# Batch 0 of an attention and expert kernel: offsets placed behind the sums of q, two scalings and a cast moved to GpSimd, an eviction to ScalarE

## The chip, the core and the metric

One core of a Trainium2 chip runs the whole kernel. TensorE (PE), VectorE (DVE), ScalarE (ACT), GpSimd (POOL) and SyncE (SP, which only issues transfers here) each work through their own list of instructions in order and wait for each other by semaphores. The metric is device microseconds (us) of one execution, lower is better. The kernel before takes 192.34 us, the median of three runs (192.24 to 192.36).

## What is computed

Linear attention over 8 batches of 8 heads, 576 rows of 64, and a mixture of 8 experts behind it, of which each row goes through one:

```python
q_s = exp(q - max(q)); q_s = q_s / (sum(q_s, -1) + 1e-09)        # over the head's 64 columns
k_s = exp(k - max(k)); k_s = k_s / (sum(k_s, over rows) + 1e-09)
kv  = einsum('bhsd,bhse->bhde', k_s, v)
x   = einsum('bhsd,bhde->bhse', q_s, kv)                          # -> 4608 rows of 512
logits = x @ w_gate + modality_bias[modality_id]
e_idx  = argmax(logits); gate = softmax(logits)[e_idx]
out[rows of e] = gate * (relu(x @ w1[e]) @ w2[e])
```

The biases make two experts win, one for each modality, and the kernel sorts rows by modality: rows of the first kind (side a) fill `xs` from the front, rows of the other (side b) from the back. A check at the end redoes rows if that was not so.

## The kernel before

**The stages of a batch.** ACT takes the exponential of q in place (`eq`, in two halves of the heads), DVE sums it over 64 columns (`sq`, L914), inverts the sums (`iq`, L925 and L926), and five instructions scale q into bf16 (`nq`, L930: four of 128x512 and one of 128x256, named by the first of their columns of rows: 0, 2, 4, 6, 8). ACT takes the exponential of k (`ekk`, L941); two instructions cast v to bf16 (`cv`, L951). TensorE multiplies k and v (`kv`, L1044, two parts), DVE scales the products into `kvbd` (`ki`, `kb`, L1071 to L1080). TensorE transposes and sorts the scaled q with a permutation (`s1`, L1130; the permutation `perm`, L959, is made by DVE), ACT or DVE evicts each group (`ev`, L1142 or L1144, into `et`), TensorE multiplies by `kvbd` (`s2`, L1169), and `put` (L1200) copies 64 columns at a time to their places in `xs`, on ACT for side a and on DVE for side b in the first two batches.

**The offsets.** Where a column group begins in `xs` is data: `off_run` scans the counts of side a (`ahead_n`, a part of the PSUM tile `own`) and packs the offsets into `offp` (L706 to L723); `lo0` loads them into registers of ACT and DVE (L1097); `aoff_run` copies `ahead_n` to SBUF (L727) for GpSimd, which can only then make the bias table (`bsel`, L757 to L762) and the places of rows (`slot`, L733 to L738).

**The experts.** For side a and b in turn, TensorE makes logits (`lg`, L1246), the hidden layer (`h`, L1318; L1312 clears a bank for the first one, which is split in two) and the output (`y`, L1331). The weights (`W`) come by transfers that GpSimd issues (`wi00` to `wi03` for the first expert, L533 and L544; `wi10` to `wi13` for the second), the first of them not before q of batch 1 has landed. q, k and v come by SP's queue.

**What sets the order.** `Plan.order` runs a small model of the engines with a cost for each step and the table `TUNED` of priorities; out of it comes one list, in which every step has an engine and a planned start, and the list is written out as it stands. A step keeps its place behind the steps ahead of it on its engine's list. `pl.fill` puts matmuls that nobody reads (fillers, L1599) into TensorE's planned gaps before 38 us, which keep that engine busy:

```python
for o in started:
    if o.engine == "PE" and o.start < hi:
        left = o.start - free - spare
        while left > 0:
            out.append(filler)
            left -= each * (2 if o.start - spare - left < slow else 1)
        free = max(free, o.start + o.costs["PE"][0])
    out.append(o)
```

Of the kernel before, what the change touches and what calls it, by code (L numbers as in the profile page):

```python
# [16 lines left out]
ACT = mybir.ActivationFunctionType  # L17
# [13 lines left out]
def view(t, dims, off=0, parts=None):  # L31
    p0 = t.ap[0]
    if parts is None:
        return bass.AP(tensor=t.tensor, offset=t.offset + off, ap=[list(p0)] + [list(d) for d in dims])
    lo, n = parts
    return bass.AP(
        tensor=t.tensor, offset=t.offset + lo * p0[0] + off, ap=[[p0[0], n]] + [list(d) for d in dims]
    )
# [206 lines left out]
def kernel(  # L245
# [12 lines left out]
    nc = tc.nc  # L258
# [26 lines left out]
    def sb(shape, dtype, name):  # L285
        return pool.tile(shape, dtype, name=name)

    pl = Plan()
# [4 lines left out]
    n_st, n_ps, n_hT, n_y = 5, 7, 3, 6  # L293
# [15 lines left out]
    ahead_n = own[:, P + 2 * NJ * HG : P + 2 * NJ * HG + NC + 1]  # L309
    sums = [own[:, P + i * NJ * HG : P + (i + 1) * NJ * HG] for i in range(2)]  # L310

    r_st, r_ps = Ring(n_st), Ring(n_ps - 1)
# [173 lines left out]
    key = sb([P, 2], FP32, "key")  # L486
# [159 lines left out]
    aoff = sb([P, NC + 1], FP32, "aoff")  # L646
# [16 lines left out]
    bsel = sb([P, NSL, E], FP32, "bsel")  # L663
# [39 lines left out]
    def off_run(_):  # L703
        d = nc.vector
        r = ps_t[r_buf.idx]
        d.tensor_tensor_scan(  # L706
            out=ahead_n[:, 1 : NC + 1],
            data0=ones[:, 0:NC],
            data1=r[:, NC : 2 * NC],
            initial=0.0,  # L710
            op0=ALU.mult,
            op1=ALU.add,
        )
        d.tensor_copy(out=off_i, in_=ahead_n[0:1, 0:NC])
        d.scalar_tensor_tensor(
            out=offp[:, :, 0:4],
            in0=view(off_i, [[NJ, B], [2, 4]], 1),
            scalar=16,
            in1=view(off_i, [[NJ, B], [2, 4]]),
            op0=ALU.logical_shift_left,  # L720
            op1=ALU.bitwise_or,
        )
        d.tensor_copy(out=offp[:, :, 4], in_=view(ahead_n, [[NJ, B]], NJ - 1, (0, 1)))  # L723

    def aoff_run(e):
        if e == "ACT":
            nc.scalar.copy(out=aoff, in_=ahead_n)  # L727
        else:
            nc.vector.tensor_copy(out=aoff, in_=ahead_n)

    def slot_run(_):
        d = nc.gpsimd
# [113 lines left out]
    pl.follow(wg_t, o_rank)  # L846
    o_pos = pl.op({"DVE": (0.8, 0.9)}, pos_run, [o_rank, c_dve], key="pos", rank=-6, uses=[r_buf])
    o_off = pl.op({"DVE": (0.8, 1.0)}, off_run, [o_pos], key="off", rank=-5, uses=[r_buf])
    o_aoff = pl.op({**on_dve(NC), **on_act(NC)}, aoff_run, [o_off], key="aoff", rank=3)
    o_vals = pl.op({"DVE": (0.7, 0.85, True)}, vals_run, [c_dve2], key="vals", rank=14)  # L850
    o_slot = pl.op({"POOL": (1.65, 1.75, True)}, slot_run, [o_aoff], key="slot", rank=12)
# [743 lines left out]
    quiet = 38.0  # L1595
# [6 lines left out]

    with tc.manual_schedule():
        waiting = []
        for o in pl.fill(pl.order({r_ps: (quiet, n_ps - 1)}), 4.5, quiet, 0.3, 0.216, 12.7, Op({"PE": (0.216, 0.45)}, unread)):
            o.run(o.engine)
            if o.engine == "PE" and waiting:
                waiting.pop()(None)
            if o in second:
                waiting.append(second[o])  # L1610
# [7 lines left out]
    def keys():  # L1618
# [12 lines left out]
    n_ps = ps_t[0]  # L1631
# [5 lines left out]
        out=ok[:, 0:1], in0=n_ps[0:1, 0:1], scalar1=float(N) - 0.5, scalar2=None, op0=ALU.is_ge  # L1637
# [5 lines left out]
        out=ok[:, B : 2 * B - 1], in0=need, scalar=(S - 2 * P) / (2 * P), in1=so_far, op0=ALU.mult, op1=ALU.is_ge  # L1643
    )
    for i, (limit, op) in enumerate(((MID - RW, ALU.is_ge), (N - (MID - RW), ALU.is_le))):
        nc.vector.tensor_scalar(
            out=ok[:, 2 * B - 1 + i : 2 * B + i], in0=aoff_x[0:1, NC : NC + 1], scalar1=float(limit), scalar2=None, op0=op
# [5 lines left out]
        out=nrest, in0=okm, scalar1=-float(E), scalar2=float(E), op0=ALU.mult, op1=ALU.add  # L1653
# [11 lines left out]
    with tc.For_i(0, nr) as e:  # L1665
        first = nc.vector.tensor_copy(out=kcol, in_=view(wrow, [[1, 1]], e))
# [8 lines left out]
        for kd in range(KD):  # L1675
            for h2 in range(2):
                nc.sync.dma_start(
                    out=st[kd // 2][64 * h2 : 64 * h2 + 64, (kd % 2) * F : (kd % 2 + 1) * F],
                    in_=bass.AP(
                        tensor=moe_w1.tensor,  # L1680
                        offset=e * (D * F) + (4 * (kd % 2) + 2 * h2 + kd // 2) * Dh * F,
                        ap=[[F, Dh], [1, F]],
                    ),
# [3 lines left out]
        for part in range(2):  # L1687
            nc.sync.dma_start(
                out=view(st[2 + part], [[D, 4], [1, D]]),
                in_=bass.AP(  # L1690
                    tensor=moe_w2.tensor, offset=e * (F * D) + part * 4 * P * D, ap=[[D, P], [P * D, 4], [1, D]]
                ),
            )
            nc.vector.tensor_copy(
                out=W[:, 0, W2 + part * 4 * D : W2 + (part + 1) * 4 * D], in_=st[2 + part][:, 0 : 4 * D]
            )
        with tc.For_i(0, NSL) as c:
            d = nc.vector
# [3 lines left out]
            for kd in range(KD):  # L1702
                nc.tensor.matmul(
                    out=ps_t[4][:, 0:E], lhsT=xx[:, kd, :], rhs=wg_sb[:, kd, :], start=(kd == 0), stop=(kd == KD - 1)
# [12 lines left out]
            for f in range(KF):  # L1717
                for kd in range(KD):
                    nc.tensor.matmul(
                        out=ps_t[f % 3][:, 0:P],  # L1720
# [39 lines left out]
```

## Time and profile before

| | |
|---|---|
| median of three runs | 192.34 us |
| the profiled execution's own time | 192.32 us |
| its span, first to last instruction | 190.7 us |
| TensorE matmul busy | 176.8 us, 93% of the span |
| VectorE busy | 143.7 us, 75% |
| ScalarE busy | 126.6 us, 66% |
| GpSimd busy | 101.8 us, 53% |
| mean granted TensorE clock | 0.991 |

The profile gives for each engine when an instruction began and how long it took. Shares of the whole span say little about one stage; the change touches the stretch from 9 to 30 us alone, so the timelines of that stretch are what to read, engine by engine, with the time that an engine stood idle before a row in brackets and who ended it.

### The profile page before, as it was taken

The page shows a single profiled execution, that of the slowest core. Times are in us where ns is not written, and L with a number is a line of the kernel's source. Part 1 is how long each engine was busy: PE and PEld are TensorE (multiplying, and loading weights), DVE is VectorE, ACT ScalarE, POOL GpSimd, SP SyncE. Part 2 cuts the span into 40 slices and gives each one's busy share as a digit, 9 for nine tenths or more (in the row PEclk, how much of TensorE's full clock was granted, in tenths as well). Part 3 has the DMA queues.
Part 4 walks back from the last instruction along what each step waited for, and adds up shares of the span by engine and source line. Part 5 has one row for each costly group of instructions (what it writes and reads, how often), then busy time and mean ns, then how long its engine had stood idle before and what let it go on. Part 6 is the DMA issues. An engine that isn't in the chain of part 4 may idle for free.

```text
span 190.7 us, 4965 instructions
## 1 busy us (share of the span) xinstructions
PE 176.8 (93%) x1743; PEld 123.7 (65%) x1759; DVE 143.7 (75%) x381; ACT 126.6 (66%) x251; POOL 101.8 (53%) x130
## 2 busy tenths in 40 slices
PE   1889799999999999999999999999999999999970
PEld 0535458587794687579668865895895975664740
DVE  4798987999989686659889899796596764363750
ACT  2655996989657299999899697599589971100000
POOL 7048989096817749844738924554831204504441
PEclk9999999999999999999999999999999999999996
DMA  5999999999999999999996683100210301412202
GB/s 196 331 401 391 270 177 213 221 375 366 195 336 383 398 410 409 397 402 406 354 389 221 258 302 115 55 5 0 111 59 0 115 0 55 168 55 110 98 31 100
DMA packets 18077, 42.34 MB, mean 222 GB/s; under 512 B 1393, under 2 KB 1393, under 8 KB 18050
## 3 DMA queue, kind: packets, MB, share of 16 engines
q1 hardware_dynamic: 12816, 28.31, 40.7%
q0 software_dynamic: 5200, 13.64, 24.8%
q8 instruction: 14, 0.23, 0.5%
q10 hardware_dynamic: 34, 0.05, 0.2%
q14 instruction: 13, 0.11, 0.2%
HBM read 36.75 MB, written 9.70 MB: 244 GB/s over the span
## 4 chain that ended last, share of the span: by engine, by line
PE 82%; DMA 7%; ACT 4%; DVE 3%; issue 2%; POOL 1%; ACTq 0%
PE ps L1318 33%; PE ps L1331 32%; DMA st<-in_v_dram 5%; PE ps L1044 5%; PE ps L1130 4%; PE ps L1169 3%; PE ps L1246 2%; DMA mraw<-in_moe_modality_id_dram 1%; ACT vb L951 1%; ACT xs L1200 1%; PE ps L1484 1%; ACT et L1142 1%; PE ps L1515 1%; DVE own L914 1%; PE ps L808 1%
## 5 line engine op out<-in xcount | busy, mean ns | idle before, releaser
L1318 PE MATMUL ps<-xs,W 128*128 128x256 bf16 x576 | 68.4, 273 | 0.1
L1331 PE MATMUL ps<-W,hT 128*128 128x512 bf16 (+1 forms) x281 | 64.8, 373 | 0.9
L1291 POOL DMA_INDIRECT out_dram<-y_sb,idx x36 | 35.5, 986 | 52.9 <-DVE y_sb L1288 39.9
L1318 PEld LDWEIGHTS <-W 128*128 128x128 bf16 x576 | 54.4, 98 | 7.7 <-issue 1.4
L1331 PEld LDWEIGHTS <-hT 128*128 128x128 bf16 x296 | 28.2, 98 | 29.1 <-issue 0.2
L930 POOL TENSOR_TENSOR eq<-st,qi 128x512 bf16<-128x512 f32 (+1 forms) x38 | 36.0, 973 | 12.1 <-PE ps L1169 4.5
L1288 DVE TENSOR_SCALAR y_sb<-ps,gate 128x512 f32<-128x512 f32 (+1 forms) x30 | 22.0, 732 | 19.5 <-PE ps L1331 14.8
L1200 ACT CAST xs<-ps 128x256 f32 (+1 forms) x90 | 28.8, 437 | 2.6 <-PE ps L1169 1.1
L1282 DVE TENSOR_SCALAR hT<-ps 128x512 bf16<-128x512 f32 x35 | 23.8, 686 | 5.4 <-PE ps L1318 3.8
L914 DVE TENSOR_REDUCE own<-st 128x18 f32<-128x1152 f32 x16 | 21.7, 1355 | 3.8 <-ACT st L908 3.7
L1280 ACT ACTIVATE hT<-ps 128x512 bf16<-128x512 f32 x37 | 21.4, 605 | 3.0 <-PE ps L1318 2.1
L908 ACT ACTIVATE st<-st 128x1152 f32<-128x1152 f32 x16 | 18.5, 1178 | 5.7 <-issue 3.4
L941 ACT ACTIVATE ek<-st 128x1152 bf16<-128x1152 f32 x16 | 18.8, 1177 | 2.7 <-DMA st<-in_k_dram 2.7
L1200 DVE CAST xs<-ps 128x256 f32 (+1 forms) x54 | 19.9, 416 | 0.5 <-issue 0.2
L1142 ACT CAST et<-ps 128x512 bf16<-128x512 f32 (+1 forms) x30 | 15.8, 555 | 5.6 <-PE ps L1130 4.5
L951 POOL CAST vb<-st 128x1152 bf16<-128x1152 f32 x8 | 9.1, 1150 | 8.8 <-DMA st<-in_v_dram 8.8
L1599 PE MATMUL ps<-ones 128*128 128x512 bf16 x39 | 12.6, 448 | 1.2 <-POOL ones L340 1.2
L1130 PE MATMUL ps<-perm,eq 128*128 128x128 bf16 x144 | 12.5, 219 | 1.0 <-POOL eq L930 0.8
L1169 PE MATMUL ps<-et,kvbd 128*128 128x128 bf16 (+1 forms) x160 | 11.8, 214 | 0.2
L1130 PEld LDWEIGHTS <-eq 128*128 128x128 bf16 x144 | 9.6, 98 | 3.7 <-POOL eq L930 1.3
L1169 PEld LDWEIGHTS <-kvbd 128*128 128x128 bf16 x160 | 10.0, 98 | 2.6 <-issue 0.6
L1044 PEld LDWEIGHTS <-ek 64*128 64x128 bf16 x288 | 8.5, 93 | 4.3 <-issue 2.8
(143 smaller groups left out, 168.6 us busy)
## 6 DMA issues: line engine op xcount, KB each, us to landing
st<-in_k_dram SPq DMA_DIRECT2D x5, 1152.0 KB, 9.7
st<-in_v_dram SPq DMA_DIRECT2D x5, 1152.0 KB, 21.4
st<-in_q_dram SPq DMA_DIRECT2D x5, 1152.0 KB, 9.2
st<-in_q_dram SPq DMA_DIRECT2D x6, 576.0 KB, 5.4
st<-in_k_dram SPq DMA_DIRECT2D x6, 576.0 KB, 7.3
st<-in_v_dram SPq DMA_DIRECT2D x6, 576.0 KB, 9.9
W<-in_moe_w_dram POOLq DMA_DIRECT2D x8, 256.0 KB
W<-in_moe_w_dram POOLq DMA_DIRECT2D x4, 512.0 KB
```

Source lines behind the costliest of these rows:

```text
L914: nc.vector.tensor_reduce(out=sums[qib.idx][:, h * NJ : (h + n) * NJ], in_=view(st[bq.idx], [[Dh, n * NJ], [1, Dh]], h * NJ * Dh), op=ALU.add,
L930: (nc.vector if e == "DVE" else nc.gpsimd).tensor_tensor(out=view(eq[eqb.idx], [[HG * Dh, n], [Dh, HG], [1, Dh]], j0 * HG * Dh), in0=view( ...
L941: nc.scalar.activation(out=view(ek[ekb.idx], [[Dh, n], [HG * Dh, NJ], [1, Dh]], h * Dh), in_=view(st[bk.idx], [[NJ * Dh, n], [Dh, NJ], [1, ...
L1130: nc.tensor.matmul(out=view(t, [[2 * nj * 64, 2], [1, 64]], hp * nj * 64 + jj * 64), lhsT=eq[eqb.idx][:, j0 + jj, P * hp : P * hp + P], rh ...
L1169: nc.tensor.matmul(out=view(ps_t[xbuf.idx], [[1, nj * 64]], c * nj * 64), lhsT=kvbd[kvb.idx][:, c, :], rhs=et[etb.idx][:, c, j0 * 64 : (j0 ...
L1200: w_ = nc.scalar.copy(out=dst, in_=src) if e == "ACT" else nc.vector.tensor_copy(out=dst, in_=src)
L1280: nc.scalar.activation(out=dst, in_=src, func=ACT.Relu)
L1282: nc.vector.tensor_scalar_max(out=dst, in0=src, scalar1=0.0)
L1288: nc.vector.tensor_scalar(out=dst, in0=src, scalar1=g, scalar2=None, op0=ALU.mult)
L1291: s_ = nc.gpsimd.indirect_dma_start(out=out, out_offset=bass.IndirectOffsetOnAxis(ap=ix[:, c : c + 1], axis=0), in_=ysb, in_offset=None, b ...
L1318: m = nc.tensor.matmul(out=t[:, i * w : (i + 1) * w], lhsT=w1(W[:, slot_, :], kd, f), rhs=xs[:, kd, lo : lo + w], start=(kd == 0 and kds = ...
L1331: nc.tensor.matmul(out=t, lhsT=h[:, kf, i * P : (i + 1) * P], rhs=W[:, slot_, W2 + kf * D + c0 : W2 + kf * D + c0 + cn], start=(kf == 0), ...
```

## The change

The plan is computed as before and then edited by hand. `aoff_run` does nothing any more; its copy stands at the end of `off_run`, so it is always VectorE's.

- On DVE the offsets come right behind the second sum of q of batch 0, then the inverse of the sums, then the permutations.
- The register load of the offsets on ACT comes right behind the second exponential of k, ahead of the cast of v.
- `nq0.6` and `nq0.8` go from DVE to GpSimd, and so does `cv1.1`, the second half of the cast of v of batch 1, from ACT. `ev0.2` goes from DVE to ACT.
- On GpSimd the five scalings of batch 0 stand together, then the issues of the first expert's weights, then `bsel`, then the cast, then `slot`.
- `ev0.4`, `ev0.6`, `s1_0.4`, `s1_0.6`, `s1_0.8` and the `s2_0` groups move forward, three of them to another PSUM bank, and new planned starts change where fillers stand. From `s2_0.8` on every planned start is 0.6 us earlier.

Nothing that belongs to later batches changes its place on its engine.

```diff
+        d.tensor_copy(out=aoff, in_=ahead_n)
+
+    def aoff_run(_):
+        pass
-    def aoff_run(e):
-        if e == "ACT":
-            nc.scalar.copy(out=aoff, in_=ahead_n)
-        else:
-            nc.vector.tensor_copy(out=aoff, in_=ahead_n)
...
+        todo = pl.order({r_ps: (quiet, n_ps - 1)})
+        def put_behind(o, first):
+            todo.remove(o)
+            todo.insert(todo.index(first) + 1, o)
+        def run_of(*keys):
+            for x, y in zip(keys, keys[1:]):
+                a, b = (k if isinstance(k, Op) else at(k) for k in (x, y))
+                put_behind(b, a)
...
+        run_of("sq0.2", o_off, "iq0", "perm0")
+        run_of("ekk0.2", lo_a)
+        for k in ("nq0.6", "nq0.8", "cv1.1"):
+            at(k).engine = "POOL"
+        at("ev0.2").engine = "ACT"
+        run_of("nq0.2", "nq0.4", "nq0.6", "nq0.8", "wi00", "wi01", "wi02", "wi03", "bsel")
+        cv = at("cv1.1")
+        todo.remove(cv)
+        todo.insert(todo.index(o_slot), cv)
+        run_of("ev0.0", "ev0.2")
+        run_of("kb0", "ev0.4")
+        run_of("kb0", "s2_0.0", "s2_0.2", "s1_0.6", "s1_0.8")
...
+        for o in todo[todo.index(at("s2_0.8")) :]:
+            o.start -= 0.6
+        for k, t in (
+            ("s1_0.4", 16.1), ("s2_0.0", 17.35), ("s2_0.2", 17.57), ("s1_0.6", 17.8), ("s1_0.8", 18.1),
```

GpSimd, from the cast of v of batch 0 (`vb_72`) to the first weights; `eq_70` is the scaled q of batch 0. Lines of the new kernel are two smaller from L724 on:

```order
-L951 CAST vb_72<-st_65 128x2x9x64
-L930 TENSOR_TENSOR eq_70<-st_63,qi_89 128x512 x2
-L757 TENSOR_SCALAR isb<-place,aoff 128x36
-L758 TENSOR_TENSOR bsel<-isb,biasd 128x288
-L761 TENSOR_TENSOR bsel<-bsel,bias_b 128x288
-L762 TENSOR_SCALAR krow<-isb,keyd,key 128x36
-L930 TENSOR_TENSOR eq_70<-st_63,qi_89 128x512
+L949 CAST vb_72<-st_65 128x2x9x64
+L928 TENSOR_TENSOR eq_70<-st_63,qi_89 128x512 x4
+L928 TENSOR_TENSOR eq_70<-st_63,qi_89 128x256
```

Two scalings have come to GpSimd, and the four instructions of the bias table have left this place. GpSimd again, between the first expert's six weight transfers and the second expert's; `vb_73` is the cast v of batch 1:

```order
+L755 TENSOR_SCALAR isb<-place,aoff 128x36
+L756 TENSOR_TENSOR bsel<-isb,biasd 128x288
+L759 TENSOR_TENSOR bsel<-bsel,bias_b 128x288
+L760 TENSOR_SCALAR krow<-isb,keyd,key 128x36
+L949 CAST vb_73<-st_64 128x2x9x64
+L731 TENSOR_TENSOR slot<-na,kt 128x72
+L732 TENSOR_TENSOR slot<-slot,pos 128x72
+L733 TENSOR_TENSOR slot<-slot,aoff 128x72
+L736 COPY slot_145<-slot 64x36 x2
```

Before, only the instructions of `slot` stood here; behind them, in both kernels, come four weight transfers (L533) and the five scalings of batch 1 (`eq_71`).

DVE, from the second sum of q on, before:

```order
L914 TENSOR_REDUCE own<-st_63 128x18
L959 TENSOR_TENSOR perm_78<-own,posx 128x1152
L925 TENSOR_SCALAR qi_89<-own 128x36
L926 RECIPROCAL qi_89<-qi_89 128x36
L706 SCALAR_TENSOR_TENSOR own<-ones,ps_95 128x72
L714 CAST off_i<-own 1x72
L715 SCALAR_TENSOR_TENSOR offp<-off_i 1x8x4
L723 CAST offp<-own 1x8
L959 TENSOR_TENSOR perm_79<-own,posx 128x1152
L1097 TENSOR_LOAD offp
```

and now:

```order
L912 TENSOR_REDUCE own<-st_63 128x18
L706 SCALAR_TENSOR_TENSOR own<-ones,ps_95 128x72
L714 CAST off_i<-own 1x72
L715 SCALAR_TENSOR_TENSOR offp<-off_i 1x8x4
L723 CAST offp<-own 1x8
L724 COPY aoff<-own 128x73
L923 TENSOR_SCALAR qi_89<-own 128x36
L924 RECIPROCAL qi_89<-qi_89 128x36
L957 TENSOR_TENSOR perm_78<-own,posx 128x1152
L957 TENSOR_TENSOR perm_79<-own,posx 128x1152
```

The offsets and the new copy `aoff` have passed the first permutation and the inverse.

## Rows read from the trace of the kernel before

**Rows 1.** The chain of waits from 24 to 36 us: start us, us, what.

```profile
25.93 0.69 PE ps L1044 x18
...
30.10 0.22 PE ps L1130 x4
```

**Rows 2.** Busy time of TensorE in a stretch: us, busy (instructions), clock, DMA share, GB/s.

```profile
36.00:186.00 150.00, 148.07 (x1471) 1.00 0.60 213
```

**Rows 3.** Timeline of POOL, 12 to 34 us: start, us, instruction, [idle before].

```profile
12.27 1.14 POOL L951 CAST vb<-st 128x1152 bf16<-128x1152 f32 x1 [7.71 <-DMA st<-in_v_dram]
13.38 2.07 POOL L930 TENSOR_TENSOR eq<-st,qi 128x512 bf16<-128x512 f32 x2
16.18 0.38 POOL L757 TENSOR_SCALAR isb<-place,aoff 128x36 f32<-128x36 f32 x1 [0.73 <-ACT aoff L727]
...
18.51 1.05 POOL L930 TENSOR_TENSOR eq<-st,qi 128x512 bf16<-128x512 f32 x1
19.52 2.69 POOL L533 DMA_DIRECT2D W<-in_moe_w_dram  x4
22.15 1.51 POOL L544 DMA_DIRECT2D W<-in_moe_w_dram  x2
23.61 0.42 POOL L733 TENSOR_TENSOR slot<-na,kt 128x72 f32<-128x72 f32 x1
...
25.51 0.65 POOL L533 DMA_DIRECT2D W<-in_moe_w_dram  x1
26.48 1.79 POOL L533 DMA_DIRECT2D W<-in_moe_w_dram  x3 [0.32 <-issue]
28.34 4.68 POOL L930 TENSOR_TENSOR eq<-st,qi 128x512 bf16<-128x512 f32 x5
```

**Rows 4.** Timeline of TensorE, 28 to 40 us.

```profile
29.94 0.39 PE L1130 MATMUL ps<-perm,eq 128*128 128x128 bf16 x4
...
31.47 0.50 PE L1130 MATMUL ps<-perm,eq 128*128 128x128 bf16 x6
...
33.45 0.39 PE L1130 MATMUL ps<-perm,eq 128*128 128x128 bf16 x4
...
35.01 3.61 PE L1331 MATMUL ps<-W,hT 128*128 128x512 bf16 x15
```

**Rows 5.** Timeline of DVE, 9 to 23 us.

```profile
9.66 1.35 DVE L914 TENSOR_REDUCE own<-st 128x18 f32<-128x1152 f32 x1
...
12.54 0.38 DVE L926 RECIPROCAL qi<-qi 128x36 f32<-128x36 f32 x1
...
13.38 1.09 DVE L715 SCALAR_TENSOR_TENSOR offp<-off_i 1x32 int32<-1x32 int32 x1
14.41 0.15 DVE L723 CAST offp<-own 1x8 int32<-1x8 f32 x1
...
21.14 0.68 DVE L930 TENSOR_TENSOR eq<-st,qi 128x512 bf16<-128x512 f32 x1
```

**Rows 6.** Timeline of ACT, 13 to 28 us.

```profile
13.74 1.16 ACT L951 CAST vb<-st 128x1152 bf16<-128x1152 f32 x1 [1.85 <-DMA st<-in_v_dram]
...
17.13 0.58 ACT L1142 CAST et<-ps 128x512 bf16<-128x512 f32 x1 [1.05 <-DVE et L1144]
17.61 2.22 ACT L908 ACTIVATE st<-st 128x1152 f32<-128x1152 f32 x2
...
24.72 2.21 ACT L951 CAST vb<-st 128x1152 bf16<-128x1152 f32 x2
```

**Rows 7.** Timeline of TensorE, 9 to 20 us (L1599 are fillers).

```profile
9.61 3.17 PE L1599 MATMUL ps<-ones 128*128 128x512 bf16 x7
...
15.80 2.54 PE L1599 MATMUL ps<-ones 128*128 128x512 bf16 x11
...
19.62 0.40 PE L1130 MATMUL ps<-perm,eq 128*128 128x128 bf16 x4 [0.83 <-POOL eq L930]
```

**Rows 8.** Transfers issued from 10.2 to 11.0 us: queue, count, size, us to landing.

```profile
st<-in_v_dram SPq DMA_DIRECT2D x1, 576.0 KB, 11.1
```

More of the change, by code (lines that the diff above doesn't have):

```diff
@@ L1604, with at @@
         waiting = []
-        for o in pl.fill(pl.order({r_ps: (quiet, n_ps - 1)}), 4.5, quiet, 0.3, 0.216, 12.7, Op({"PE": (0.216, 0.45)}, unread)):
+        todo = pl.order({r_ps: (quiet, n_ps - 1)})
+        def at(key, n=0):
+            return [o for o in todo if o.key == key][n]
+        def put_behind(o, first):
[5 more added lines that the diff above has]
+                put_behind(b, a)
+        lo_a = at("lo0", [o.engine for o in todo if o.key == "lo0"].index("ACT"))
+        run_of("sq0.2", o_off, "iq0", "perm0")
[10 more added lines that the diff above has]
+        run_of("kb0", "s2_0.0", "s2_0.2", "s1_0.6", "s1_0.8")
+        run_of("ev0.4", "s2_0.4")
+        run_of("put00.2", "ev0.6", "s2_0.6")
+        run_of("s1_0.2", "s1_0.4")
+        for k, bank in (("s1_0.4", 2), ("s2_0.2", 0), ("s2_0.6", 2)):
+            at(k).takes[0].idx = bank
+        for o in todo[todo.index(at("s2_0.8")) :]:
+            o.start -= 0.6
+        for k, t in (
+            ("s1_0.4", 16.1), ("s2_0.0", 17.35), ("s2_0.2", 17.57), ("s1_0.6", 17.8), ("s1_0.8", 18.1),
+            ("s2_0.4", 18.6), ("s2_0.6", 20.3), ("s2_0.8", 21.5),
+        ):
+            at(k).start = t
+        for o in pl.fill(todo, 4.5, quiet, 0.3, 0.216, 12.7, Op({"PE": (0.216, 0.45)}, unread)):
             o.run(o.engine)
```

## The prediction

> **What bounds the kernel now.** I began at the far end. From 36 to 186 us TensorE is busy for 148.07 of 150 us at granted clock 1.00 [rows 2], so behind 36 us there are 1.93 us of idle time in all, and whatever delay TensorE has there stays in the end to nearly its full size. The question is thus when TensorE gets to a fixed place near 30 us. The place I take is the first sorting of batch 1 (`s1`, four instructions at 29.94): the chain of waits passes it, at 30.10, after `kv` at 25.93 [rows 1]. Behind it come the other sortings, and at 35.01 the long output multiplication `y` [rows 4].
>
> The sorting reads what GpSimd scaled. GpSimd's five scalings of batch 1 begin at 28.34 and take 4.68 us, 0.94 each on average [rows 3]. A first one as long as the one alone at 18.51 (1.05) ends at 29.39, and TensorE reads it at 29.94: 0.55 us of slack. All five are done at 28.34 + 4.68 = 33.02, and the last group is sorted at 33.45: 0.43 us. For the middle one I take 28.34 + 1.05 + 0.94 + about 0.65 (two more, one of half size, at the mean of the five: half of 0.94 is 0.47, and 0.94 + 0.47 = 1.41; only the half one stands ahead of the sorting at 31.47), that is about 31.0, 0.5 us ahead [rows 3, 4]. So GpSimd is 0.4 to 0.6 us from being the bound, and the change makes its list longer ahead of just this place.
>
> **GpSimd, the term that decides.** Both kernels start the scalings of batch 0 at 13.38, behind the cast of `v`, if `iq` is ready then. From there to the scalings of batch 1 its list holds, before, 28.34 − 13.38 = 14.96 us [rows 3]. The new list, priced by the same rows:
> - five scalings at what the five of batch 1 took, 4.68: to 18.06. Before, three were here (2.07 + 1.05, with the overlap of rows 3.08), so 1.60 are added.
> - six issues of weights, 23.61 − 19.52 = 4.09: to 22.15.
> - the bias table, four instructions, 18.51 − 16.18 = 2.33: to 24.48. The 0.73 us of idle time ahead of it, for the copy of `aoff`, is gone.
> - the cast `cv1.1`, at what the cast of batch 0 took, 13.38 − 12.27 = 1.11: to 25.59.
> - `slot`, 25.51 − 23.61 = 1.90: to 27.49.
> - four issues, 28.34 − 25.51 = 2.83: to 30.32.
>
> So the scalings of batch 1 begin 1.98 us later (1.60 + 1.11 − 0.73). Take off the slack: the first sorting is 1.98 − 0.55 = 1.43 late, the third about 1.5, the last 1.98 − 0.43 = 1.55. I take 1.5 us.
>
> Both ends of this term: 0.32 us in the four issues is idle time that the profile calls "issue" [rows 3]; if it goes, the term is 1.2. If all ten issues cost what the last three did (1.79/3 = 0.60 each, 6.0 in place of 4.09 + 2.83 = 6.92), it is 0.6. Upwards, five scalings at the 1.05 of the one alone (four and a half of them, 4.73) and a cast at 1.14 add under 0.1, and the wait for `v` that comes below up to 1.3.
>
> **VectorE.** The four offset instructions and the new copy pass ahead of the first permutation and the inverse. The sums end at 9.66 + 1.35, about 11.05. Of the offset instructions L715 is the long one: 1.09 us for 32 numbers, while its neighbour L723 took 0.15, and it ended about when GpSimd's first scaling of 1.04 (13.38 to 14.41) did [rows 3, 5]. [...]
>
> If L715 is as short as L723, then the offsets with the copy take about 1.0: the first two stand between 12.54 + 0.38 = 12.92 and 13.38, 0.46; L715 and L723 at 0.15 each; an estimate of 0.25 for the copy, which reads little more than the first two. The inverse, 0.38 and about 0.2 for the small instruction ahead of it, ends near 11.05 + 1.0 + 0.6 = 12.65, against 12.92 before: nothing waits. If it takes 1.09 again, `iq` comes at about 13.6, GpSimd starts 0.2 to 0.25 us late and the whole term grows by that. I take zero, as GpSimd is idle there until 12.27, and keep 0.25 for the range. The two scalings that leave VectorE (0.68 at 21.14, and one of half size) give it 1.1 us in a stretch where it is not the bound at 30 us, so I count nothing for them.
>
> **ScalarE and the front of TensorE.** The register load now sits in the 1.85 us of idle time ahead of the cast of `v` (13.74); the copy of `aoff` leaves. The cast ends at 14.90. Two evictions follow in place of one at 17.13: the first is ready behind the sorting of the first scaling, the second after GpSimd's second scaling (13.38 + 2.07 = 15.45), 0.39 of sorting and 0.58 of evicting, so to about 16.5. The exponentials of batch 1's q, at 17.61 before, then begin 1.1 us sooner. The second half of the cast of batch 1 (half of 2.21, begun about 24.72 + 1.1 = 25.8) leaves too [rows 6]. So ScalarE's chain, and `kv` at 25.93 with it, moves 0.6 to 1.1 us forward: the lower end is the planned 0.6 of the diff, the upper this sum.
>
> That gain is real but does not reach the end: TensorE would arrive at the sorting at about 29.94 − 0.8 = 29.1, and the first scaled q is there at 30.32 + 1.05 = 31.37. It stands for about 2.3 us, and leaves 1.43 late however soon it came. The fillers need no term of their own for that reason: they lie ahead of this wait. Behind the sorting the work of batch 1 and the experts runs as before, 1.5 us later, and since only 1.93 of 150 us are idle, I give back nothing; a fifth of it, 0.3, is the bound downwards.
>
> **The transfer of v.** `cv1.1` now waits for the second half of `v` of batch 1 on GpSimd, with `slot`, four issues and all scalings of batch 1 behind it. The first half landed 11.1 us after an issue between 10.2 and 11.0 [rows 8], 21.3 to 22.1. Of the second half the trace only says that ScalarE's cast found it at about 25.8, without a wait. Here it is wanted at 24.48. The wait lies between 0 and 1.3; nearest is the landing of the first half, so I take 0. The first weights are issued 1.46 us sooner (18.06 against 19.52) and share the transfer engines with this tail. [...]
>
> **The sum.** 192.32 (the profiled execution, 0.02 under the median) + 1.5 = **193.8 us**, slower.
>
> **Rivals.**
> - *GpSimd is quick enough, and the front's gain wins.* If VectorE's work next to GpSimd stretches its instructions, the new order, with scalings together and VectorE relieved of two, might run them faster. The calculations ahead of 28.34 (4.68 + 2.33 + 1.11) would have to cost about 1.9 us less in 8.1, under 77% of their rows; from there TensorE no longer waits and the gain of 0.6 to 1.1 counts: 191.2 to 191.7. Against it: scalings took 0.94, 1.04 and 1.05 in three places with very different work on VectorE. Chance 0.07.
> - *It does less than it says, in both directions.* The issues cost 0.60 and the 0.73 and 0.32 of idle time go, some of the cast's place too: GpSimd is late by under 1 us, and TensorE by at most 0.4, 192.1 to 192.7. Chance 0.08.
> - *`v` is late on GpSimd.* Another wait of 0.6 to 1.3 at the cast, in full on the path: 194.4 to 195.1. For it: the transfers begin sooner. Against: 2.4 to 3.2 us lie between the first half's landing and the need. Chance 0.11.
> - *The pause lowers TensorE's clock.* [...] Chance 0.10.
>
> **How the numbers follow.** The main case has 0.64: 193.4 to 194.3 around 193.8, from 1.2 less a little given back to 1.5 plus 0.25 for `iq` and 0.2 for small things. 192.7 to 195.1 takes in the upper end of the same-time case, the 0.6 end of the issues, the whole main case and the late `v`; outside are the faster rival, most of the clock rival and part of the second. What a measurement of this kernel can tell from no change is about 0.2%, 0.4 us. Faster by more than that 0.08, within it 0.07, slower 0.85.
>
> **What would show it.** Right: GpSimd's list as above, `slot` ending near 27.5, the first scaling of batch 1 near 30.3; TensorE idle for some 2 us ahead of the sorting, with GpSimd's `eq` named as the releaser, and `y` near 36.5. L715 short and ScalarE's exponentials at about 16.5 confirm the front. Wrong: scalings of batch 1 that begin before 28.9 (then the slack covers it), idle time ahead of the cast on GpSimd (`v`), a clock under 1.00 in the stretch after 30 us, or TensorE arriving at the sorting later than before, which would mean that the front lost time too.

## The result, and the profile after

The changed kernel takes 194.49 us in the middle of its runs, against 192.34: the ratio is 1.0112, with a 95% interval of 1.0088 to 1.0135. That is 1.1% slower, inside the range (192.7 to 195.1), and 0.7 above the forecast of 193.8. The medians below hold every execution; the ratios leave out those that took over 1.5% more than the fastest of their kernel (here 196.22 and 196.66 us, with mean clocks of 0.976 and 0.988), so a ratio can leave out part of what a fallen clock costs. The kernel before has its middle at 192.34 us here and at 191.86 to 192.22 beside the experiments, so each experiment is compared with its own runs of the kernel before.

The profiled execution took 195.79 us (span 194.2), one of the longer ones. GpSimd first: its timeline, with the columns of [rows 3].

```profile
11.76 1.14 POOL L949 CAST vb<-st 128x1152 bf16<-128x1152 f32 x1 [7.50 <-DMA st<-in_v_dram]
13.81 4.68 POOL L928 TENSOR_TENSOR eq<-st,qi 128x512 bf16<-128x512 f32 x5 [0.91 <-DVE qi L924]
18.44 2.68 POOL L533 DMA_DIRECT2D W<-in_moe_w_dram  x4
...
22.55 0.46 POOL L755 TENSOR_SCALAR isb<-place,aoff 128x36 f32<-128x36 f32 x1
...
24.94 1.15 POOL L949 CAST vb<-st 128x1152 bf16<-128x1152 f32 x1
26.06 0.33 POOL L731 TENSOR_TENSOR slot<-na,kt 128x72 f32<-128x72 f32 x1
...
28.27 2.47 POOL L533 DMA_DIRECT2D W<-in_moe_w_dram  x4 [0.52 <-issue]
30.80 4.67 POOL L928 TENSOR_TENSOR eq<-st,qi 128x512 bf16<-128x512 f32 x5
```

From the first scaling of batch 0 to the first of batch 1 this list takes 30.80 − 13.81 = 16.99 us. It was 14.96 before [rows 3], and 14.96 + 1.98 = 16.94 was forecast. But it also begins 0.43 later, at 13.81, behind 0.91 us of idle time that VectorE's inverse (L924) ended. Together the scalings of batch 1 are 2.46 us late.

TensorE's timeline, to be laid beside [rows 1, 4]:

```profile
25.82 0.68 PE L1042 MATMUL ps<-vb,ek 64*128 64x129 bf16 x18
...
29.38 0.61 PE L1316 MATMUL ps<-xs,W 128*128 128x256 bf16 x4
31.91 0.61 PE L1128 MATMUL ps<-perm,eq 128*128 128x128 bf16 x4 [1.92 <-POOL eq L928]
32.31 2.77 PE L1316 MATMUL ps<-xs,W 128*128 128x256 bf16 x12
34.87 0.69 PE L1128 MATMUL ps<-perm,eq 128*128 128x128 bf16 x6
...
38.60 3.61 PE L1329 MATMUL ps<-W,hT 128*128 128x512 bf16 x16
```

The sorting begins at 31.91 in place of 29.94 (+1.97), after 1.92 us of pause for GpSimd's `eq`. Then a second loss: the 12 multiplications behind it take 2.77 us. The same row in TensorE's timeline before, and the windows of both kernels (us, busy and instructions, granted clock, DMA share, GB/s), before first:

```profile
30.16 1.47 PE L1318 MATMUL ps<-xs,W 128*128 128x256 bf16 x12
```

```profile
26.00:36.00 10.00, 9.82 (x122) 1.00 1.11 203
```

```profile
26.00:36.00 10.00, 8.08 (x86) 0.83 1.12 209
```

The granted clock fell from 1.00 to 0.83 in this stretch: in the changed kernel it is 1.00 from 26 to 29.9 us, 0.50 behind the pause, from 31.9 to 34.9, and 0.87 from 35 to 36, and 2.77 − 1.47 = 1.30 us went there. With the sortings on both sides it is a little more: from the first sorting to `y` it is 38.60 − 31.91 = 6.69 us, before 35.01 − 29.94 = 5.07 [rows 4], a loss of 1.62. `y` is thus 1.97 + 1.62 = 3.59 later than before. From there to the end it is 195.79 − 38.60 = 157.2 us, before 192.32 − 35.01 = 157.3: nothing is given back.

VectorE and ScalarE at the front:

```profile
9.87 1.35 DVE L912 TENSOR_REDUCE own<-st 128x18 f32<-128x1152 f32 x1
...
11.86 1.08 DVE L715 SCALAR_TENSOR_TENSOR offp<-off_i 1x32 int32<-1x32 int32 x1
12.87 0.15 DVE L723 CAST offp<-own 1x8 int32<-1x8 f32 x1
...
13.29 0.38 DVE L924 RECIPROCAL qi<-qi 128x36 f32<-128x36 f32 x1
```

```profile
14.33 1.16 ACT L949 CAST vb<-st 128x1152 bf16<-128x1152 f32 x1 [2.93 <-DVE qi L924]
...
17.07 2.22 ACT L906 ACTIVATE st<-st 128x1152 f32<-128x1152 f32 x2
...
24.11 1.16 ACT L949 CAST vb<-st 128x1152 bf16<-128x1152 f32 x1
```

L715 took 1.08 us again, and ended with GpSimd's cast (11.76 + 1.14 = 12.90). The inverse is therefore late, and so is ScalarE: its register load waits for the offsets, begins at 13.1 and holds the cast of `v` behind it until 14.33, against 13.74 in [rows 6].

### The profile page after: what moved, and what is told of

It is laid out like the page before. It is cut to its first block, busy times and chain, and to the rows that moved or that the text cites. A ratio compares the mean times of both kernels' runs of the same rounds, so it can differ in the third digit from the quotient of the medians.

```text
span 194.2 us, 4985 instructions
## 1 busy us (share of the span) xinstructions
PE 179.7 (93%) x1759; PEld 124.9 (64%) x1759; DVE 142.8 (74%) x379; ACT 126.7 (65%) x250; POOL 104.1 (54%) x133
## 4 chain that ended last, share of the span: by engine, by line
PE 79%; POOL 8%; DVE 4%; issue 3%; DMA 2%; ACT 1%; POOLq 0%; ACTq 0%
PE ps L1316 32%; PE ps L1329 32%; PE ps L1128 4%; PE ps L1042 4%; PE ps L1167 3%; DMA st<-in_q_dram 2%; PE ps L1244 2%; POOL W L533 2%; POOL eq L928 2%; DVE own L912 1%; PE ps L1482 1%; PE ps L1513 1%; POOL W L544 1%; ACT st L906 1%; PE ps L806 1%
## 5 line engine op out<-in xcount | busy, mean ns | idle before, releaser
L1316 PE MATMUL ps<-xs,W 128*128 128x256 bf16 x576 | 69.6, 276 | 0.1
L1329 PE MATMUL ps<-W,hT 128*128 128x512 bf16 (+1 forms) x296 | 65.7, 373 | 0.1
L1316 PEld LDWEIGHTS <-W 128*128 128x128 bf16 x576 | 55.2, 99 | 8.1 <-issue 1.1
L928 POOL TENSOR_TENSOR eq<-st,qi 128x512 bf16<-128x512 f32 (+1 forms) x40 | 37.6, 967 | 14.7 <-PE ps L1167 4.5
L1140 ACT CAST et<-ps 128x512 bf16<-128x512 f32 (+1 forms) x31 | 16.4, 554 | 8.2 <-PE ps L1128 8.0
L949 POOL CAST vb<-st 128x1152 bf16<-128x1152 f32 x9 | 10.2, 1151 | 7.5 <-DMA st<-in_v_dram 7.5
L1263 ACT ACTIVATE ex<-L,gmx 128x8 f32<-128x8 f32 x36 | 8.7, 297 | 5.5 <-DVE gmx L1259 3.4
```

Source lines behind the costliest of these rows:

```text
L928: (nc.vector if e == "DVE" else nc.gpsimd).tensor_tensor(out=view(eq[eqb.idx], [[HG * Dh, n], [Dh, HG], [1, Dh]], j0 * HG * Dh), in0=view( ...
L1316: m = nc.tensor.matmul(out=t[:, i * w : (i + 1) * w], lhsT=w1(W[:, slot_, :], kd, f), rhs=xs[:, kd, lo : lo + w], start=(kd == 0 and kds = ...
L1329: nc.tensor.matmul(out=t, lhsT=h[:, kf, i * P : (i + 1) * P], rhs=W[:, slot_, W2 + kf * D + c0 : W2 + kf * D + c0 + cn], start=(kf == 0), ...
```

## Experiments

The theories: **A**, GpSimd's longer list delays the sorting, and the pause that this opens lowers TensorE's clock in some executions. **B**, the clock falls for a reason of its own. **C**, the new turns of batch 0 and the offsets cost the time, and GpSimd is only the last to be named. only_pool, only_pool_fill, only_off and off_cv0 start from the kernel before, the others from the changed one. Line numbers of only_pool and only_pool_fill are those of the kernel before.

All times in the table are from the profiled executions: when GpSimd's scalings of batch 1 begin, when the sorting of batch 1 begins, TensorE's pause right ahead of it, and the granted clock from 26 to 36 us. In cv_act and cv0_act the pause that counts lies earlier, as told below.

| kernel | ratio to before | interval | scalings | sorting | pause | clock |
|---|---|---|---|---|---|---|
| before | 1 | | 28.34 | 29.94 | 0 | 1.00 |
| changed | 1.0112 | 1.0088 to 1.0135 | 30.80 | 31.91 | 1.92 | 0.83 |
| after_again | 1.0125 | 1.0079 to 1.0172 | 30.54 | 31.64 | 1.95 | 0.83 |
| only_pool | 1.0152 | 1.0110 to 1.0195 | 30.82 | 31.93 | 2.11 | 0.83 |
| only_pool_fill | 1.0104 | 1.0080 to 1.0127 | 30.33 | 31.63 | 0 | 1.00 |
| fill8 | 1.0115 | 1.0088 to 1.0141 | 30.09 | 31.20 | 0.28 | 1.00 |
| iq_first | 1.0067 | 1.0043 to 1.0092 | 30.44 | 31.55 | 1.75 | 0.83 |
| cv0_act | 1.0147 | 1.0102 to 1.0193 | 30.59 | 31.71 | 0 | 0.83 |
| nq_dve | 1.0090 | 1.0043 to 1.0138 | 30.83 | 31.94 | 3.07 | 0.86 |
| cv_act | 1.0025 | 1.0007 to 1.0043 | 28.44 | 31.71 | 0 | 0.83 |
| no_pool | 0.9996 | 0.9972 to 1.0020 | 27.90 | 29.66 | 0 | 1.00 |
| only_off | 0.9975 | 0.9942 to 1.0008 | 27.78 | 29.14 | 0 | 1.00 |
| off_cv0 | 1.0000 | 0.9979 to 1.0022 | 27.53 | 29.50 | 0 | 1.00 |
| best | 0.9989 | 0.9968 to 1.0010 | 27.52 | 29.18 | 0 | 1.00 |

### The change taken apart: A or C

**only_pool**, the kernel before with the three moves to GpSimd alone:

```diff
...
+        for k in ("nq0.6", "nq0.8", "cv1.1"):
+            at(k).engine = "POOL"
+        run_of("nq0.4", "nq0.6", "nq0.8")
+        cv = at("cv1.1")
+        todo.remove(cv)
+        todo.insert(todo.index(o_slot), cv)
...
```

> The kernel before with three moves alone: the last two scalings of batch 0 on GpSimd, behind the third, and the second half of the cast of v of batch 1 on GpSimd, ahead of slot. No other order is changed. Theory A: GpSimd's list ahead of the scalings of batch 1 grows by 1.60 + 1.11 = 2.7 us, to about 31.0; less 0.5 of slack the sorting is 2.2 late, and TensorE pauses for about 2 us: 194.5, and up to 1.5 more where the clock falls. Theory C (the turns of batch 0 and the offsets are what costs): nothing of these is here, so about 192.3.

195.56 us in the middle. The moves alone cost no less than the whole change, as A had it. GpSimd and then TensorE in this kernel:

```profile
13.09 2.07 POOL L930 TENSOR_TENSOR eq<-st,qi 128x512 bf16<-128x512 f32 x2
...
30.82 4.68 POOL L930 TENSOR_TENSOR eq<-st,qi 128x512 bf16<-128x512 f32 x5
```

```profile
31.93 0.40 PE L1130 MATMUL ps<-perm,eq 128*128 128x128 bf16 x4 [2.11 <-POOL eq L930]
32.16 2.54 PE L1318 MATMUL ps<-xs,W 128*128 128x256 bf16 x12
...
38.62 1.67 PE L1331 MATMUL ps<-W,hT 128*128 128x512 bf16 x7
```

The list is 30.82 − 13.09 = 17.73 us long. Here the wait for the copy of `aoff` is still in it, and 14.96 + 1.60 + 1.11 = 17.67 would be the prediction's sum. From the sorting to `y` it is 6.69 us again.

**no_pool**, the changed kernel without these three moves, the rest kept:

```diff
-        for k in ("nq0.6", "nq0.8", "cv1.1"):
-            at(k).engine = "POOL"
...
-        run_of("nq0.2", "nq0.4", "nq0.6", "nq0.8", "wi00", "wi01", "wi02", "wi03", "bsel")
-        cv = at("cv1.1")
-        todo.remove(cv)
-        todo.insert(todo.index(o_slot), cv)
+        run_of("nq0.2", "nq0.4", "wi00", "wi01", "wi02", "wi03", "bsel")
...
+        run_of("kb0", "nq0.6", "nq0.8")
```

> The changed kernel without its three moves to GpSimd: the last two scalings of batch 0 on VectorE behind its products for kvbd, the second half of the cast of v of batch 1 on ScalarE. The offsets, the eviction on ScalarE and the turns of batch 0 stay. Theory A: GpSimd's list is 2.7 us shorter than in the changed kernel, its scalings of batch 1 begin at 27.5 to 28.3, no pause ahead of the sorting: 191.5 to 192.4. The front's gain shows only as far as the first expert's weights have landed, which is about 26.3 to 27.4 in all runs so far, whether they were issued at 17.0 or at 18.4. Theory C: the turns cost, and the time stays at about 194.5.

192.32, no different from before: the new turns, the eviction and the offsets cost nothing, and bring nothing. GpSimd and then TensorE:

```profile
27.90 4.69 POOL L928 TENSOR_TENSOR eq<-st,qi 128x512 bf16<-128x512 f32 x5
```

```profile
29.66 0.39 PE L1128 MATMUL ps<-perm,eq 128*128 128x128 bf16 x4
```

**only_off**, the kernel before with only the offsets, the copy and the register load moved:

```diff
+        d.tensor_copy(out=aoff, in_=ahead_n)
...
+        lo_a = at("lo0", [o.engine for o in todo if o.key == "lo0"].index("ACT"))
+        run_of("sq0.2", o_off, "iq0", "perm0")
+        run_of("ekk0.2", lo_a)
...
```

> The kernel before with the offsets alone moved: right behind the second sum of q on VectorE, with the copy of aoff on VectorE at their end, and ScalarE's register load behind its second exponential of k. Theory A: GpSimd's 0.73 us of idle time ahead of its bias table goes, so its scalings of batch 1 could begin at about 27.6, but the inverse of batch 1's sums is ready no sooner than 27.9, and TensorE is not held by GpSimd: 191.9 to 192.5. Theory C: slower, by 0.5 or more.

192.02; the interval (0.9942 to 1.0008) allows a gain of half a per cent and also none. C falls with these three runs. Only in no_pool, only_off and the two last kernels of the table does GpSimd begin before 28.34, and only there is the sorting no later than before.

**after_again** is the changed kernel beside these runs.

> The changed kernel once more, beside the runs that follow, on the same chip. Theory A: GpSimd's scalings of batch 1 begin 1.7 to 2.5 us later than 28.34 (the lower end where L715 is short, as it was wherever VectorE reached it before GpSimd began its cast), ratio to the kernel before 1.008 to 1.013, and executions with a lower mean clock (under 0.990) are about 1.5 us slower than the rest.

1.0125, the same as at first, and L715 at 0.95 us. Two of its six executions, with a mean clock of 0.986, took 195.39 and 196.58, the other four 194.31 to 194.55.

### The clock: A or B

**fill8**, fillers in the pause of the changed kernel, and **only_pool_fill**, nine of them in that of only_pool:

```diff
+        filler = Op({"PE": (0.216, 0.45)}, unread)
+        todo = pl.fill(todo, 4.5, quiet, 0.3, 0.216, 12.7, filler)
+        n = todo.index(at("s1_1.0"))
+        todo[n:n] = [filler] * 8
...
```

> The changed kernel with eight more fillers on TensorE, right ahead of the first sorting of batch 1, in the 1.92 us for which it stood idle there. Nothing else. Theory A (GpSimd's longer list delays that sorting, and the pause ahead of it lowers TensorE's clock in some executions): eight fillers of 0.22 us fill 1.7 of the 1.92 us, the sorting starts as late as before the fillers (31.9), the granted clock is 1.00 from 26 to 36 us, the 12 multiplications behind the sorting take about 1.5 us in place of 2.77, and the time is about 193.8, with a narrower spread than 193.2 to 196. Theory B (the clock falls for a reason of its own, not for the pause): the clock falls as without the fillers, 194.5 in the middle, with the same spread. Theory C (the front of TensorE is what is late, not GpSimd): eight fillers are in the way, and the time grows by up to 1.7, 196.

> The kernel with the three moves to GpSimd alone (195.56 in the middle, ratio 1.0152, mean clock under 0.990 in five executions of six), and nine more fillers on TensorE ahead of the first sorting of batch 1, in the 2.11 us that it stood idle there. Theory A (the pause lowers the clock): the sorting starts as late as without them, the clock from 26 to 36 us is 1.00, no execution's mean clock is under 0.990, and the ratio falls by 0.005 to 0.008, to about 1.008 to 1.010 (193.9). Theory B (the clock falls for another reason): the ratio stays at 1.015.

TensorE in fill8, then in only_pool_fill:

```profile
29.03 1.89 PE L1597 MATMUL ps<-ones 128*128 128x512 bf16 x8
31.20 0.40 PE L1128 MATMUL ps<-perm,eq 128*128 128x128 bf16 x4 [0.28 <-POOL eq L928]
31.43 1.47 PE L1316 MATMUL ps<-xs,W 128*128 128x256 bf16 x12
```

```profile
29.69 2.10 PE L1599 MATMUL ps<-ones 128*128 128x512 bf16 x9
31.63 0.39 PE L1130 MATMUL ps<-perm,eq 128*128 128x128 bf16 x4
31.85 1.47 PE L1318 MATMUL ps<-xs,W 128*128 128x256 bf16 x12
...
36.70 3.61 PE L1331 MATMUL ps<-W,hT 128*128 128x512 bf16 x16
```

The sorting is as late as GpSimd makes it, but the 12 multiplications are back at 1.47 us, and in only_pool_fill it is 36.70 − 31.63 = 5.07 us from the sorting to `y`, as before the change. Work that nobody reads has taken the ratio of only_pool from 1.0152 to 1.0104, as A said (1.008 to 1.010 was expected). The two intervals still overlap, but the clocks do not: the mean clock of only_pool was under 0.990 in five executions of six, and with the fillers in none (0.992 to 0.998). Of the kernels that have the pause ahead of the sorting, and that ran beside the two with fillers, iq_first went under 0.990 in two executions of seven and nq_dve in five of nine. So B does not explain this fall. In the kernel before, whose profile has no such pause, the mean clock can be low too: it is 0.975 to 0.983 in three of the 66 executions beside these experiments.

For the changed kernel the middle hardly moves (1.0115 beside 1.0112 and 1.0125; 194.07 us, where 193.8 was expected), because only some of its executions lose the clock: of the twelve in its ratio, four have a mean clock of 0.986 or 0.987 (194.41 to 195.79) and eight one of 0.992 to 0.998 (193.20 to 194.51). With the fillers all six lie between 193.83 and 194.77. So the wait alone is worth about 1.9 of the 2.15 us in the middle (the eight have theirs at 194.2), and the clock about 1.2 us more, between the middles of the two groups, in a third of the executions.

### L715 and the start of GpSimd's list

**cv0_act**: GpSimd's half of the cast of `v` of batch 0 goes to ScalarE, and GpSimd does nothing while VectorE makes the offsets.

```diff
+        at("cv0.0").engine = "ACT"
+        run_of("ekk0.2", "cv0.0", lo_a)
-        run_of("ekk0.2", lo_a)
```

> The changed kernel with GpSimd's half of the cast of v of batch 0 on ScalarE, ahead of the register load: GpSimd does nothing until the inverse of batch 0 is there. If L715 is slow because GpSimd works next to it: L715 takes 0.15 to 0.2 in place of 1.08, the inverse ends at about 12.8, the scalings of batch 0 begin there, 1.0 us sooner, and the time is about 193.2 by theory A. If L715 is slow by itself: 1.08 again, the scalings begin at about 13.7 as before, 194.4. Theory C: unchanged at 194.5 or later, as ScalarE is busier by 1.16 us at the front.

**iq_first**: the inverse of the sums ahead of the offsets.

```diff
-        run_of("sq0.2", o_off, "iq0", "perm0")
+        run_of("sq0.2", "iq0", o_off, "perm0")
```

> The changed kernel with VectorE's inverse of the sums ahead of the offsets, so that GpSimd's scalings of batch 0 need not wait for the offsets. Theory A: the scalings of batch 0 begin right behind GpSimd's cast, about 12.95 in place of 13.81 or at the least 0.4 us sooner, all of GpSimd's list moves by that, and the time falls by 0.4 to 0.9: 193.6 to 194.1. On L715: if it is slow because GpSimd is working next to it, it now stands beside GpSimd's scalings and takes about 1.1 again, ending with a scaling. Theory C: 194.5, since the offsets come later and the front with them.

L715 in cv0_act, and then in fill8, where GpSimd's cast happened to begin at 11.78, just behind it:

```profile
11.84 0.18 DVE L715 SCALAR_TENSOR_TENSOR offp<-off_i 1x32 int32<-1x32 int32 x1
```

```profile
11.55 0.18 DVE L715 SCALAR_TENSOR_TENSOR offp<-off_i 1x32 int32<-1x32 int32 x1
```

L715 is not slow by itself. It took 0.18 us in six profiles in which GpSimd stood idle when it ran (also cv_act, nq_dve, off_cv0 and best), and 0.78 to 1.09 in the others, where a cast or scaling of GpSimd was under way, and then it ended with that. In the changed kernel it varies from execution to execution which comes first: in its two profiles and that of fill8 VectorE gets to L715 at 11.86, 11.70 and 11.55, and the cast of `v` begins at 11.76, 11.46 and 11.78. Both kernels of this group start GpSimd's list earlier, at 12.89 and 12.37. What became of that shows on GpSimd further on, in cv0_act and then in iq_first:

```profile
24.84 1.15 POOL L949 CAST vb<-st 128x1152 bf16<-128x1152 f32 x1 [0.75 <-DMA st<-in_v_dram]
```

```profile
24.57 1.15 POOL L949 CAST vb<-st 128x1152 bf16<-128x1152 f32 x1 [1.01 <-DMA st<-in_v_dram]
```

The cast `cv1.1` waits for `v` of batch 1, which lands at about 24.6 to 24.8, and most of the gain at the start is lost there: of 0.92 us in cv0_act and 1.44 in iq_first, 0.21 and 0.36 are left when the scalings of batch 1 begin. iq_first came out at 193.41 in the middle, ratio 1.0067, the upper end of what it was expected to gain, though its profiled execution is its slowest (195.22; the other six are 192.99 to 193.62), so the waits of the ordinary ones aren't seen. cv0_act missed its 193.2: 194.62, with the cast's wait and one more that the next group shows.

### One move at a time

**cv_act**, the cast `cv1.1` back on ScalarE, and **nq_dve**, the two scalings back on VectorE; each is the part of no_pool's diff that names these steps.

> The changed kernel with the second half of the cast of v of batch 1 back on ScalarE. Theory A: GpSimd's list is 1.15 us shorter, its scalings of batch 1 begin at 29.65 in place of 30.80, the sorting at about 30.8, the pause is under 0.9 us and the clock stays; ScalarE's second half ends by about 26.4, as before, so kv doesn't wait. About 193.1. Theory C (the front): time unchanged at about 194.5, or worse by up to 1.1 as ScalarE gets the cast back.

> The changed kernel with the last two scalings of batch 0 on VectorE, behind its products for kvbd; the second half of the cast of v of batch 1 stays on GpSimd. Theory A: GpSimd's list is 1.6 us shorter than in the changed kernel and 0.4 longer than before, and with L715 long its scalings of batch 1 begin at about 29.2, unless v is awaited: the cast is wanted at 23.3 and its data landed as late as 24.6 to 24.8 in two executions, so a wait of up to 1.4 stands ahead of it and the scalings begin by 30.5. Time 192.8 to 193.9, the upper part where GpSimd stands idle ahead of the cast. Theory C: 194.5.

GpSimd in nq_dve, and TensorE:

```profile
25.07 1.15 POOL L949 CAST vb<-st 128x1152 bf16<-128x1152 f32 x1 [2.03 <-DMA st<-in_v_dram]
```

```profile
31.94 0.40 PE L1128 MATMUL ps<-perm,eq 128*128 128x128 bf16 x4 [3.07 <-POOL eq L928]
```

Taking 1.6 us of scalings off GpSimd's list brought little: the cast stood idle for 2.03 us until `v` was there, and the scalings of batch 1 began at 30.83, as in the changed kernel. Its nine executions spread from 192.8 to 196.4, so part of them may wait less; their middle, 195.48, misses the 192.8 to 193.9 that was expected, and five of them have a mean clock under 0.990.

With the cast gone instead (cv_act), the list is free of that landing:

```profile
12.65 4.68 POOL L928 TENSOR_TENSOR eq<-st,qi 128x512 bf16<-128x512 f32 x5
...
28.44 4.68 POOL L928 TENSOR_TENSOR eq<-st,qi 128x512 bf16<-128x512 f32 x5
```

The list is 15.79 us long in place of 16.99, shorter by the cast. That is half of the 2.36 us by which the scalings of batch 1 are sooner; the other 1.16 stand at the start of the list: L715 was short in this profile, and the sums began 0.68 sooner than in the changed kernel's (9.19 against 9.87). The ratio is 1.0025, and the middle of 192.75 is the 193.1 of A or slightly better. The one move that costs most is the cast: it puts a transfer's landing at the middle of GpSimd's list.

In the profiled execution of cv_act (193.75, above its middle) another limit comes up:

```profile
27.44 0.98 PE L1316 MATMUL ps<-xs,W 128*128 128x256 bf16 x4 [1.51 <-DMA W<-in_moe_w_dram]
...
31.71 0.39 PE L1128 MATMUL ps<-perm,eq 128*128 128x128 bf16 x4
```

TensorE gets to the first hidden layer early and waits 1.51 us for the first expert's weights, although GpSimd issued them from 17.28 on, 2.24 us sooner than in [rows 3]. In cv0_act it is the same (1.22 us, to 27.44, issued from 17.52). The four multiplications behind the pause take 0.98 us in place of 0.61, and the granted clock is 0.83 from 26 to 36 us in both kernels.

### Looking for a better kernel

**off_cv0** is only_off and **best** is no_pool, both with GpSimd's cast of batch 0 on ScalarE as in cv0_act, so that L715 is short.

> The kernel before with the offsets moved (ratio 0.9975 by itself), and GpSimd's half of the cast of v of batch 0 on ScalarE, so that GpSimd is idle while VectorE makes the offsets. L715 takes 0.18, the inverse ends at about 12.7, GpSimd's scalings of batch 0 begin there, 0.8 us sooner. GpSimd is not the bound at the sorting in that kernel (27.78 against a need of 28.3 or so), so the gain can only come through the front of TensorE and ScalarE's register load: 191.4 to 192.2, ratio 0.995 to 1.000, by the weights' landing no lower.

> The changed kernel without its three moves to GpSimd and with GpSimd's half of the cast of v of batch 0 on ScalarE: the offsets, the eviction on ScalarE and the turns of batch 0 stay, L715 takes 0.18, and the front is some 0.7 us sooner than in the same kernel with GpSimd's cast (192.32, ratio 0.9996). If the front is what holds TensorE: 191.6. If the first weights' landing at 26.3 to 27.4 does: TensorE waits for them, idle time up to 1.5 us stands ahead of the first hidden layer, and the time is 192.0 to 192.4, or more where that pause lowers the clock.

191.73 and 191.60, ratios 1.0000 and 0.9989, both no different from before. In off_cv0 TensorE waits for the weights as well:

```profile
26.72 0.60 PE L1316 MATMUL ps<-xs,W 128*128 128x256 bf16 x4 [0.67 <-DMA W<-in_moe_w_dram]
```

An earlier front runs into the weights' landing, between 26.2 and 27.5 in the six profiles that waited for it (26.26 in fill8 at the earliest), with issues that began anywhere from 16.99 to 20.34. Among these, issuing sooner did not bring the weights sooner; nq_dve, which issued from 16.46 on, began its hidden layer at 25.93 without a wait for them. Why was not tried. The windows show a DMA share of 1.10 or 1.11 from 17 to 26 us in the five of the six that issued by 18.24, and one of 0.90 in only_pool_fill, which issued last.

## Why the prediction was right, and where it was off

- **GpSimd's list** was the right term, and its sum was right to 0.05 us (16.99 against 16.94). only_pool and no_pool show that it alone is the loss.
- **The start of that list** is the term that was mis-sized: zero was taken for a late inverse, and the list began 0.43 later. The step that failed is "I take zero, as GpSimd is idle there until 12.27". The cast begins when `v` lands, and that was 11.76 here, ahead of L715, which took 1.08. Not all of the 0.43 is L715: in this execution the sums began at 9.87, against 9.66 in [rows 5], and 0.21 came from there. The other 0.22 is what the prediction had named for a long L715 (0.2 to 0.25). That L715 is short beside an idle GpSimd is what the runs show (0.18 against 0.78 to 1.09); that GpSimd would be idle did not hold, because it hung on a landing time.
- **The slack** of 0.55 held: 2.46 late on GpSimd, 1.97 on TensorE. In the middle one of its three slacks the prediction adds 0.65 for a half-size scaling that it prices at 0.47; by its own price the end is 30.80 and the slack 0.67, and nothing hung on it.
- **The clock** was put as a rival of its own (chance 0.10). The longest pause of the kernel before from 9 to 40 us is 0.83 [rows 7], so that chance was the author's estimate. A fallen clock is no alternative to the wait but comes on top of it, in a third of the executions; in the profiled one it took 1.62 us from the sorting to `y`. A clock under 1.00 in the stretch after 30 us was also named as a sign of being wrong, and it came: 0.72 from 30 to 36 us.
- **`v` late on GpSimd** did not happen in the changed kernel's profile, where the cast began at 24.94 without a wait. It was within a few tenths of being the bound: it landed at 24.57 to 25.07 in the three profiles in which GpSimd's cast waited for it (iq_first, cv0_act, nq_dve). Zero was taken since the first half's landing was the nearest row; 24.48 and the 25.8 of ScalarE's cast were the bounds, and the landings lie in the lower half between them. As for the transfer engines that the weights share with `v`: from 15 to 32 us the packets of the profile's queues q0 and q1 took 67.1% and 38.7% of the time of the same 16 engines before, 71.5% and 38.1% in the changed kernel. What the sooner weights cost `v` is not shown.
- **The front** gained nearly nothing (`kv` at 25.82 against 25.93; 0.6 to 1.1 forecast). ScalarE was 0.54 sooner at the exponentials (17.07) and 0.61 at the cast of batch 1 (24.11), not 1.1, as the late offsets held its register load and the cast behind it. TensorE did not take even that: it stood 1.32 us for an eviction of VectorE's, until 23.48, and then ran nine fillers, 2.11 us (rows in the last section); whether `kv` could have begun sooner without these is not shown. The gain would have been swallowed anyway: at the sorting, as predicted, or ahead of it at the weights, which had not been seen.
- **Give-back**: none, as forecast.

The forecast of 193.8 is 0.7 low. The eight executions that kept the clock have their middle at 194.2, 0.4 above it. That is the size of the late start in the profile, but no profile shows it for these eight. The rest is what the clock takes in the other four. The result lies above the main case (193.4 to 194.3). It is inside the range by the part that was kept for a late `v`, which neither profile of the changed kernel shows; that much is luck.

## What to carry to other kernels

Sum the whole list of the engine that gets the work, from the moved step to the next step that somebody waits for, and compare with the slack there: here 2.0 us against 0.5. Ask of each step moved to another engine which transfer it waits for, and what then stands behind that wait: in nq_dve the cast waited 2.03 us for `v`, and the scalings of batch 1 began no sooner than in the changed kernel (30.83 against 30.80). A pause that is unavoidable can be filled with matmuls that nobody reads; here the granted clock from 26 to 36 us was 1.00 with them (fill8, only_pool_fill) and 0.83 without, and they did nothing about the wait itself.

## What the runs showed of the hardware

- VectorE's L715, an instruction on 32 numbers, took 0.18 us with GpSimd idle and 0.78 to 1.09 with a GpSimd cast or scaling under way, ending with it (at 12.94 against 12.90 in the changed kernel). GpSimd's cast took 1.14 us beside it there and 1.14 without it in fill8. No row shows GpSimd as the one that waits.
- TensorE's granted clock was 0.83 to 0.86 from 26 to 36 us in the profiled executions with a pause of 1.22 us (cv0_act), 1.51 (cv_act) or 1.75 to 3.07 ahead of the sorting. It was 1.00 from 17 to 20 us before, around the pause of 0.83 [rows 7], and from 17 to 26 us in best, which has a pause of 0.87. The length of one pause is not all of it: the changed kernel has one of 1.32 us, and the nine fillers behind it run at 2.11/9 = 0.23 us each, at a granted clock of 1.00 from 23.4 to 25.6.

```profile
23.48 0.28 PE L1167 MATMUL ps<-et,kvbd 128*128 128x64 bf16 x4 [1.32 <-DVE et L1142]
23.59 2.11 PE L1597 MATMUL ps<-ones 128*128 128x512 bf16 x9
```

- Weights that GpSimd issued from 16.99 to 20.34 us on landed at 26.26 to 27.44 us, in no order of their issues, in the six profiles that waited for them.
